# Load order of the first batch, load timing of the later ones, and the last stores of a fused attention and expert kernel

## The chip, the cores and the metric

The kernel runs on one core of a Trainium2 chip. The metric is the time of one execution in device microseconds (us); lower is better. Two kinds of number appear: the **time** of plain executions (a median of several), and the **span** of one profiled execution, from its first instruction to its last, about 2 us shorter. The sets of rounds ran on different chips, so a kernel is compared with the kernel before of its own set where that is possible.

PE is the matmul engine and PEld its weight loads, DVE the vector engine, ACT the scalar engine, POOL the general engine whose queue issues the loads, SP the engine whose queue issues DMA transposes and stores.

## The reference

Four batches of cross-covariance attention (queries and keys are normalised along the sequence, so the attention matrix is 256 x 256), followed by a feed-forward network without activation functions:

```python
B, N, C = (4, 5824, 256)
qn = q / (np.linalg.norm(q, axis=1, keepdims=True) + 1e-06)
kn = k / (np.linalg.norm(k, axis=1, keepdims=True) + 1e-06)
s = kn.transpose(0, 2, 1) @ qn / tau
a = softmax(s)                      # over the last axis
x = (v @ a).reshape(B * N, C)
h = ((x @ w1) * (x @ w2)) @ w3      # d_ff = 1024
out = h @ w_out
```

(The softmax is shortened here.) The kernel folds `a` into w1 and w2 once for each batch (the "folds", giving `Wf`), and w3 into w_out once (`W_sb`), so that the long part is two products `a` and `b` of v with `Wf`, their elementwise product, and one output product `o`.

## The kernel before

The engines' programs are laid out by hand: Python code puts steps on an agenda by a model clock (`at(t, cost, fn)`), and each engine executes its own list in order. A wait on one engine holds back everything behind it on that engine.

The first batch has nothing to overlap with. Its loads all go through POOL's queue, and PE does squares (for the norms) and products (for G) as pieces land:

```python
for pi in range(1, 4):
    load_piece("k", 0, pi)
    load_piece("q", 0, pi)
load_piece("k", 0, 4)
load_piece("k", 0, 5)
# ... PE: squares and products of pieces 0 to 3
load_piece("q", 0, 4, (half,))
load_piece("q", 0, 5, (2, 4))
for h in range(2):                  # expert weights, by halves of their columns
    nc.gpsimd.dma_start(out=w12[:, :, 0, hs], in_=w1r[:, :, hs])
    nc.gpsimd.dma_start(out=w12[:, :, 1, hs], in_=w2r[:, :, hs])
    # ... half h of v piece 0
squares("k", 4, whole)
squares("k", 5, range(LAST + 1), end=True)
soft0[0]()                          # DVE: diagonal of k's squares
busy(2)
soft0[1]()                          # the k row: PE, then four ACT steps
# ... PE: squares and products of q pieces 4 and 5, softmax up to e
soft0[3]()
busy(4)                             # warm-up matmuls, into the wait for e
transpose_half_on_pe(0, 0, 0, False)
soft0[4]()                          # row sums of e, folds 0 to 5
```

In the later batches loads and transposes lie on the agenda. `gate` makes POOL wait for current work of PE, ACT and DVE, and `hold` makes it wait for a DMA transpose of v; `hold` is used only in batch 0:

```python
moves = [("v", b, 3, 1.0), ("qk", n, 0, 4.0), ("qk", n, 1, 12.0), ...]
if before is not None and b == 0:
    at(t, 0.0, lambda w=before: hold(...))
at(t, 0.0, gate)
```

The last, small chunk of a batch has one tile of 128 rows and, in every second batch, a second one with the 64 left-over rows of two batches. Both go into one PSUM tile:

```python
nc.scalar.copy(o[:, 0, :], tl[0][:, 0, :])
(nc.scalar if b == B - 1 else nc.sync).dma_start(out=rows[:, NT - 1, :], in_=o[:, 0, :])
if b % 2 == 1:
    nc.vector.tensor_copy(o[:, 1, :], tl[0][:, 1, :])
    for k in range(2):
        nc.sync.dma_start(out=..., in_=o[k * LEFT : (k + 1) * LEFT, 1, :])
```

Of the kernel before, what the change touches and what calls it, by code (L numbers as in the profile page):

```python
# [12 lines left out]
F32 = DT.float32  # L13
BF16 = DT.bfloat16

P = 128
# [8 lines left out]
def kernel(  # L25
# [12 lines left out]
    nc = tc.nc  # L38

    B, N, C = q.shape  # L40
    T, D = out.shape
# [8 lines left out]
    FT = F // P  # L50
    NT = N // P
    LEFT = N - NT * P
    assert LEFT == 64 and NT % 4 == 1
    NP_ = (NT + PIECE - 1) // PIECE
    LAST = NT - (NP_ - 1) * PIECE
# [57 lines left out]
    def load_piece(nm, n, pi, cuts=()):  # L113

        new_piece(nm, n, pi)
        ends = [0, *cuts, LAST if pi == NP_ - 1 else PIECE]
        for lo, hi in zip(ends, ends[1:]):
            load_part(nm, n, pi, lo, hi)
# [86 lines left out]
    def busy(k):  # L205

        m = psum.tile([P, 512], F32, tag="ab", name=f"warm_{nc.get_next_instruction_name()}", bufs=4)
        for _ in range(k):
            nc.tensor.matmul(m, lhsT=warm[:, :P], rhs=warm, start=True, stop=True, skip_group_check=True)
# [29 lines left out]
    def soft_units(n):  # L239
# [94 lines left out]
            sum_mm(0)  # L334
            sum_mm(1)

        def fold_mm(i, c2, tag="ab"):
            h, rest = divmod(i, 4)
            w, c1 = divmod(rest, 2)
            if c2 == 0:  # L340
                st["fold", i] = psum.tile(
                    [P, 512], F32, tag=tag, name=f"fold_{n}_{i}", bufs={"ab": 4, "out": 3}[tag]
                )
            nc.tensor.matmul(  # L344
                st["fold", i], lhsT=st["e"][:, c2, c1 * P : (c1 + 1) * P], rhs=w12[:, c2, w, h * 512 : (h + 1) * 512],
                start=(c2 == 0), stop=(c2 == CT - 1),
            )
            if c2 == CT - 1:
                dst = Wf[n][:, c1, w, h * 512 : (h + 1) * 512]
                if i % 2 == 0:  # L350
                    nc.scalar.activation(out=dst, in_=st["fold", i], func=AF.Copy, scale=st["rs"][:, c1 : c1 + 1])  # L351
                else:
                    nc.vector.tensor_scalar_mul(dst, st["fold", i], st["rs"][:, c1 : c1 + 1])

        def fold(i, tag="ab"):
            fold_mm(i, 0, tag)
            fold_mm(i, 1, tag)

        def first_folds():
            sum_mm(0)  # L360
            fold_mm(0, 0)
            fold_mm(1, 0)
            sum_mm(1)
            fold_mm(0, 1)
            fold_mm(1, 1)
            fold(2)
            fold(3)
            fold(4, "out")
            fold(5, "out")

        if n == 0:
# [17 lines left out]
    def at(t, cost, fn):  # L389
        seq[0] += 1  # L390
        agenda.append((t, seq[0], cost, fn))
# [57 lines left out]
    def emit_out(b, c, j, ab):  # L449
        small = c == NCH - 1  # L450
        if small:
            lhs = [ab[:, :P]]
            if b % 2 == 1:
                lhs.append(lefts[b // 2][:, j, :, :].rearrange("p b t -> p (b t)"))
        else:
            lhs = [ab[:, i * P : (i + 1) * P] for i in range(4)]
        if j == 0:
            out_tiles[b, c] = [
                psum.tile([P, 2, D], F32, tag="out", name=f"o_{b}_{c}_{h}", bufs=3) for h in range((len(lhs) + 1) // 2)
            ]  # L460
        tl = out_tiles[b, c]
        for s, lhsT in enumerate(lhs):
            nc.tensor.matmul(  # L463
                tl[s // 2][:, s % 2, :], lhsT=lhsT, rhs=W_sb[:, j, :],
                start=(j == 0 and s % 2 == 0), stop=(j == FT - 1 and (s % 2 == 1 or s == len(lhs) - 1)),
                skip_group_check=True,
            )
        clock[0] += len(lhs) * (D * MM_COL + MM_FIX)
        if j == FT - 1:
            o = work.tile([P, 4, D], F32, tag="o_sb", name=f"osb_{b}_{c}", bufs=3)  # L470
            rows = out[b * N : b * N + NT * P, :].rearrange("(p i) c -> p i c", i=NT)
            if small:
                nc.scalar.copy(o[:, 0, :], tl[0][:, 0, :])
                (nc.scalar if b == B - 1 else nc.sync).dma_start(out=rows[:, NT - 1, :], in_=o[:, 0, :])
                if b % 2 == 1:
                    nc.vector.tensor_copy(o[:, 1, :], tl[0][:, 1, :])
                    for k in range(2):
                        m = b - 1 + k
                        nc.sync.dma_start(
                            out=out[m * N + NT * P : (m + 1) * N, :], in_=o[k * LEFT : (k + 1) * LEFT, 1, :]  # L480
                        )
            else:
                nc.scalar.copy(o[:, 0:2, :], tl[0])  # L483
                nc.vector.tensor_copy(o[:, 2:4, :], tl[1])  # L484
                nc.sync.dma_start(out=rows[:, 4 * c : 4 * c + 4, :], in_=o)
            del out_tiles[b, c]
# [8 lines left out]
    half = PIECE // 2  # L495
# [20 lines left out]
    for pi in range(1, 4):  # L516
        load_piece("k", 0, pi)
        load_piece("q", 0, pi)
    load_piece("k", 0, 4)
    load_piece("k", 0, 5)  # L520
    soft0 = soft_units(0)
    whole = range(PIECE)
# [6 lines left out]
        products(0, sl)  # L529
    for pi in range(1, 4):  # L530
        squares("k", pi, whole)
        busy(2)
        squares("q", pi, whole)
        products(pi, whole)
    load_piece("q", 0, 4, (half,))
    load_piece("q", 0, 5, (2, 4))
    for h in range(2):
        hs = slice(h * F // 2, (h + 1) * F // 2)
        nc.gpsimd.dma_start(out=w12[:, :, 0, hs], in_=w1r[:, :, hs])
# [6 lines left out]
    nc.gpsimd.dma_start(out=wout_sb, in_=moe_w_out.rearrange("(lh ll) c -> ll lh c", ll=P))  # L546
    nc.gpsimd.dma_start(out=w3_bf, in_=w3r)
    squares("k", 4, whole)
    squares("k", 5, range(LAST + 1), end=True)
    soft0[0]()  # L550
    busy(2)
    soft0[1]()
    for sl in (lo, hi):
        squares("q", 4, sl)
        products(4, sl)
    parts = [[LAST, 0, 1], [2, 3], [4]]
    for sl in parts:
        squares("q", 5, sl, end=sl is parts[-1])
        if sl is parts[-1]:
            soft0[2]()  # L560
        products(5, sl, end=sl is parts[-1])
    soft0[3]()
    busy(4)
    transpose_half_on_pe(0, 0, 0, False)
    soft0[4]()
    w_ready = [False]

# [15 lines left out]
    def make_agenda(b):  # L583
        agenda.clear()
        clock[0] = 0.0
        n = b + 1
        if b == 0:
            for i in range(2):
                at(1.5 + 0.6 * i, 0.43, soft0[5 + i])
            at(4.0, 0.5, lambda: transpose_half_on_pe(0, 0, 1, False))  # L590
            at(7.0, 0.5, lambda: transpose_half_on_pe(0, 1, 0, True))
            at(8.0, 0.5, lambda: transpose_half_on_pe(0, 1, 1, False))
            at(15.0, 0.0, transpose_w3)
            at(15.0, 0.0, lambda: transpose_piece(0, 2))
            for jt in range(FT):
                at(26.0 + 1.2 * jt, 0.87, lambda jt=jt: w_unit(jt))
            moves = [("v", 0, 3, 29.0), ("qk", 1, 0, 38.0), ("qk", 1, 1, 43.0), ("v", 0, 4, 50.0), ("qk", 1, 2, 58.0)]
            moves += [("qk", 1, 3, 63.0), ("v", 0, 5, 70.0), ("qk", 1, 4, 81.0), ("qk", 1, 5, 87.0)]
            moves += [("v", 1, 0, 96.0), ("v", 1, 1, 106.0), ("v", 1, 2, 116.0)]
            t0, t1 = 58.0, 120.0  # L600
        else:
            moves = [("v", b, 3, 1.0), ("qk", n, 0, 4.0), ("qk", n, 1, 12.0), ("v", b, 4, 20.0), ("qk", n, 2, 27.0)]
            moves += [("v", b, 5, 34.0), ("qk", n, 3, 44.0), ("qk", n, 4, 58.0), ("qk", n, 5, 72.0)]
            moves += [("v", n, 0, 84.0), ("v", n, 1, 96.0), ("v", n, 2, 108.0)]
            moves = [m for m in moves if m[1] < B]
            t0, t1 = 16.0, 104.0


        before = (0, 2) if b == 0 else None
        for nm, m, pi, t in moves:  # L610
            if before is not None and b == 0:
                at(t, 0.0, lambda w=before: hold(vTs[w[0]][1][:1, 0, :1] if w[1] == NP_ - 1 else vTs[w[0]][0][:1, w[1] * PIECE, 0, :1]))
            at(t, 0.0, gate)
            if nm == "qk":
                at(t, 0.0, lambda m=m, pi=pi: load_qk(m, pi))
                before = None
            else:
                at(t, 0.0, lambda m=m, pi=pi: load_piece("v", m, pi))
                at(t + (4.0 if b == 0 else 8.0), 0.0, lambda m=m, pi=pi: transpose_piece(m, pi))
                before = (m, pi)  # L620
        if n == B:
            agenda.sort()
            return
        units = score_units(n)
        for i, (cst, fn) in enumerate(units):
            at(t0 + (t1 - t0) * i / len(units), cst, fn)
        soft = soft_units(n)
        ts = [t1 + 1.0, t1 + 3.5, t1 + 4.0, t1 + 8.0, t1 + 12.0] + [t1 + 13.0 + 0.9 * i for i in range(8)]
        for t, (cst, fn) in zip(ts, soft):
            at(t, cst, fn)  # L630
        agenda.sort()
# [50 lines left out]
```

## Time and profile before

| quantity | value |
|---|---|
| time, median of 3 | 576.39 us (576.14 to 577.7) |
| span of the profile | 574.4 us |
| PE busy | 561.9 us, 98% |
| PE idle between 40 and 569 us | 0.86 us |
| first `a` matmul on the chain of waits | 40.66 us |
| last matmul begins / span ends | 569.59 / 574.4 us |

Most of a profile like this one, here 529 of 574 us, can be put aside at once: where the engine that sets the pace (PE) is busy without a gap, only taking work from it helps. What is left lies at the two ends. The prediction below shows the lines.

### The profile page before, as it was taken

How to read it: one execution, taken by the hardware profiler on the slowest of the kernel's cores; microseconds unless marked ns; L12 is line 12 of the kernel's file. 1: busy time of each engine (PE TensorE's matmuls, PEld its weight loads, DVE VectorE, ACT ScalarE, POOL GpSimd, SP SyncE). 2: the span in 40 equal slices, each digit the busy share in tenths (PEclk: the TensorE clock that was granted, in tenths of full speed). 3: DMA queues.
4: the chain of work that ended last, by engine and by line, in shares of the span. 5: the costliest groups of instructions: out<-in, count | busy, mean ns of one | idle time of the engine just before them, and what ended most of it. 6: DMA issues, size and time to landing. Idle time of an engine off the chain costs nothing.

```text
span 574.4 us, 10119 instructions
## 1 busy us (share of the span) xinstructions
PE 561.9 (98%) x3770; PEld 356.8 (62%) x3770; DVE 374.7 (65%) x597; ACT 338.6 (59%) x624; POOL 65.9 (11%) x147
## 2 busy tenths in 40 slices
PE   7899999999999999999999999999999999999996
PEld 4665576776666666666666666666665656666665
DVE  0047744687967567887776567778876655565564
ACT  0046534777766567776765567767765554454453
POOL 5240020302100212010000112001100000000000
PEclk9999999999999999999999999999999999999999
DMA  8999959879570997564643798654562335311011
GB/s 163 211 208 201 186 101 229 178 167 218 129 182 38 174 210 154 111 149 90 143 111 88 142 226 173 139 111 100 136 143 78 84 80 145 83 45 67 38 74 55
DMA packets 74416, 76.93 MB, mean 134 GB/s; under 512 B 54144, under 2 KB 58112, under 8 KB 74368
## 3 DMA queue, kind: packets, MB, share of 16 engines
q0 software_dynamic: 15360, 39.46, 39.5%
q1 hardware_dynamic: 58864, 36.71, 21.8%
q8 instruction: 29, 0.48, 0.3%
q14 instruction: 19, 0.16, 0.1%
q10 hardware_dynamic: 144, 0.13, 0.1%
HBM read 78.91 MB, written 23.86 MB: 179 GB/s over the span
## 4 chain that ended last, share of the span: by engine, by line
PE 90%; DMA 6%; ACT 1%; issue 1%; DVE 1%; POOL 1%; ACTq 0%; POOLq 0%
PE o L463 27%; PE a L424 27%; PE b L424 27%; PE G L188 5%; DMA q<-in_q_dram 4%; PE fold L344 2%; PE w L571 1%; DMA v<-in_v_dram 1%; ACT as L430 1%; POOL k L109 0%; DVE abs L439 0%; DVE osb L484 0%; PE row L272 0%; POOL q L109 0%; PE ss L283 0%
## 5 line engine op out<-in xcount | busy, mean ns | idle before, releaser
L439 DVE TENSOR_TENSOR abs<-as,b 128x512 bf16<-128x512 bf16 x336 | 229.9, 687 | 140.1 <-ACT as L430 128.6
L430 ACT CAST as<-a 128x512 bf16<-128x512 f32 (+1 forms) x384 | 215.8, 563 | 176.4 <-PE a L424 86.1
L424 PEld LDWEIGHTS <-Wf 128*128 128x128 bf16 x1536 | 149.1, 98 | 102.1 <-issue 2.3
L463 PE MATMUL o<-W_sb,abs 128*128 128x256 bf16 x1376 | 209.7, 273 | 0.5 <-ACT osb L483 0.4
L424 PE MATMUL a<-vT,Wf 128*128 128x512 bf16 x704 | 209.3, 379 | 0.3
L424 PE MATMUL b<-vT,Wf 128*128 128x512 bf16 x704 | 209.4, 379 | 0.0
L463 PEld LDWEIGHTS <-abs 128*128 128x128 bf16 x1376 | 134.5, 98 | 82.0 <-issue 0.6
L197 DVE TENSOR_TENSOR acc<-acc,sq 128x1024 f32<-128x1024 f32 x66 | 80.5, 1219 | 0.8 <-ACT sq L185 0.8
L188 PE MATMUL G<-k,q 128*128 128x256 bf16 x276 | 49.6, 273 | 0.0
L412 POOL COPY gate_t<-abs 1x1 bf16<-1x1 bf16 x39 | 9.7, 249 | 299.0 <-DVE abs L439 290.5
L185 ACT ACTIVATE sq<-q 128x512 f32<-128x512 bf16 x66 | 41.8, 633 | 0.0
L185 ACT ACTIVATE sq<-k 128x512 f32<-128x512 bf16 x66 | 41.6, 631 | 0.0
L484 DVE COPY osb<-o 128x512 f32<-128x512 f32 x44 | 30.1, 685 | 0.0
L188 PEld LDWEIGHTS <-q 128*128 128x128 bf16 x276 | 27.0, 98 | 3.1
L483 ACT COPY osb<-o 128x512 f32<-128x512 f32 x44 | 25.8, 586 | 4.5 <-PE o L463 2.6
L274 ACT ACTIVATE kr<-row 128x256 f32<-128x256 f32 x4 | 1.5, 384 | 31.2 <-PE row L272 31.2
L344 PE MATMUL fold<-w,e 128*128 128x512 bf16 x64 | 16.8, 378 | 0.0
L109 POOL DMA_DIRECT2D q<-in_q_dram x28 | 15.1, 539 | 14.2 <-DMA k<-in_k_dram 5.4
L351 ACT ACTIVATE Wf<-fold,rs 128x512 bf16<-128x512 f32 x16 | 10.9, 687 | 7.2 <-PE fold L344 4.9
L109 POOL DMA_DIRECT2D k<-in_k_dram x25 | 13.7, 549 | 3.4 <-DMA k<-in_k_dram 1.9
L109 POOL DMA_DIRECT2D v<-in_v_dram x25 | 13.5, 540 | 5.7 <-issue 3.9
L439 DVE TENSOR_TENSOR abq<-as,b 128x512 bf16<-128x512 bf16 x16 | 10.9, 686 | 3.9 <-ACT as L430 3.4
(89 smaller groups left out, 209.7 us busy)
## 6 DMA issues: line engine op xcount, KB each, us to landing
out_dram<-osb SPq DMA_DIRECT2D x44, 512.0 KB, 3.1
k<-in_k_dram POOLq DMA_DIRECT2D x19, 512.0 KB, 8.8
v<-in_v_dram POOLq DMA_DIRECT2D x19, 512.0 KB, 5.2
q<-in_q_dram POOLq DMA_DIRECT2D x18, 512.0 KB, 6.3
w_wout<-in_moe_w_dram POOLq DMA_DIRECT2D x1, 2048.0 KB, 22.2
k<-in_k_dram POOLq DMA_DIRECT2D x4, 320.0 KB, 8.9
v<-in_v_dram POOLq DMA_DIRECT2D x4, 320.0 KB, 5.2
q<-in_q_dram POOLq DMA_DIRECT2D x4, 256.0 KB, 10.5
```

Of the source, the lines that this page charges most:

```text
L109: nc.gpsimd.dma_start(out=pieces[nm, n, pi][:, lo:hi, :], in_=qk_main[nm, n][0][:, pi * PIECE + lo : pi * PIECE + hi, :])
L185: nc.scalar.activation(out=dst[:, :, part, :], in_=src[:, o : o + 2, :], func=AF.Square)
L188: nc.tensor.matmul(G[:, ct, :], lhsT=qt[:, i, ct * P : (ct + 1) * P], rhs=kt[:, i, :], start=(pr == 0 and part == 0 and ct == 0), stop=(pr ...
L197: nc.vector.tensor_add(accs[n], accs[n], sqs[0])
L344: nc.tensor.matmul(st["fold", i], lhsT=st["e"][:, c2, c1 * P : (c1 + 1) * P], rhs=w12[:, c2, w, h * 512 : (h + 1) * 512], start=(c2 == 0), ...
L351: nc.scalar.activation(out=dst, in_=st["fold", i], func=AF.Copy, scale=st["rs"][:, c1 : c1 + 1])
L424: nc.tensor.matmul(t[:, :n], lhsT=Wf[b][:, ct, w, j * P : (j + 1) * P], rhs=rhs_of(b, c, ct), start=(ct == 0), stop=(ct == CT - 1),)
L430: nc.scalar.copy(a_sb[:, :n], tiles[0][:, :n])
L439: nc.vector.tensor_mul(ab, a_sb, tiles[1])
L463: nc.tensor.matmul(tl[s // 2][:, s % 2, :], lhsT=lhsT, rhs=W_sb[:, j, :], start=(j == 0 and s % 2 == 0), stop=(j == FT - 1 and (s % 2 == 1 ...
L483: nc.scalar.copy(o[:, 0:2, :], tl[0])
L484: nc.vector.tensor_copy(o[:, 2:4, :], tl[1])
```

## The change

The intent: get through the first batch's data sooner by taking q and k in turn to the end; keep loads and DMA transposes of the later batches apart; and shorten the way from the last matmul to the last store. The diff, cut (marked with `...`) to its core:

```diff
         def first_folds():
...
             fold(2)
-            fold(3)
-            fold(4, "out")
+            transpose_half_on_pe(0, 0, 0, False)
+            fold(3, on_act=True)
+            fold(4, "out", on_act=False)
             fold(5, "out")
...
-                psum.tile([P, 2, D], F32, tag="out", name=f"o_{b}_{c}_{h}", bufs=3) for h in range((len(lhs) + 1) // 2)
+                psum.tile([P, 2, D], F32, tag="out", name=f"o_{b}_{c}_{h}", bufs=3)
+                for h in range(len(lhs) if small else 2)
...
-                    nc.vector.tensor_copy(o[:, 1, :], tl[0][:, 1, :])
-                    for k in range(2):
+                    o2 = work.tile([P, D], F32, tag="kr", name=f"oleft_{b}", bufs=1)
+                    nc.vector.tensor_copy(o2, tl[1][:, 0, :])
+                    for k, eng in enumerate((nc.sync, other)):
...
     load_piece("k", 0, 4)
+    load_piece("q", 0, 4, (half,))
     load_piece("k", 0, 5)
...
-    load_piece("q", 0, 4, (half,))
-    load_piece("q", 0, 5, (2, 4))
+    load_piece("q", 0, 5, (1, 3, 4))
...
     squares("k", 4, whole)
-    squares("k", 5, range(LAST + 1), end=True)
-    soft0[0]()
-    busy(2)
-    soft0[1]()
     for sl in (lo, hi):
         squares("q", 4, sl)
         products(4, sl)
-    parts = [[LAST, 0, 1], [2, 3], [4]]
+    squares("k", 5, range(LAST + 1), end=True)
+    soft0[0]()
+    parts = [[LAST, 0], [1, 2], [3], [4]]
...
+        if i == 0:
+            soft0[1]()
     soft0[3]()
     busy(4)
-    transpose_half_on_pe(0, 0, 0, False)
     soft0[4]()
...
-            if before is not None and b == 0:
+            if before is not None:
                 at(t, 0.0, lambda w=before: hold(...))
...
-                at(t + (4.0 if b == 0 else 8.0), 0.0, lambda m=m, pi=pi: transpose_piece(m, pi))
+                at(t + 4.0, 0.0, lambda m=m, pi=pi: transpose_piece(m, pi))
```

In the lists of moves for the later batches, `("qk", n + 1, 0, 108.0)` is added at the end of batch b, and the other loads move by up to 12 us.

More of the change, by code (lines that the diff above doesn't have):

```diff
@@ L335, in sums, with fold_mm @@
             sum_mm(1)
-        def fold_mm(i, c2, tag="ab"):
+        def fold_mm(i, c2, tag="ab", on_act=None):
             h, rest = divmod(i, 4)
@@ L349, in fold_mm @@
                 dst = Wf[n][:, c1, w, h * 512 : (h + 1) * 512]
-                if i % 2 == 0:
+                if on_act if on_act is not None else i % 2 == 0:
                     nc.scalar.activation(out=dst, in_=st["fold", i], func=AF.Copy, scale=st["rs"][:, c1 : c1 + 1])
@@ L353, in fold_mm, with fold @@
                     nc.vector.tensor_scalar_mul(dst, st["fold", i], st["rs"][:, c1 : c1 + 1])
-        def fold(i, tag="ab"):
+        def fold(i, tag="ab", on_act=None):
             fold_mm(i, 0, tag)
-            fold_mm(i, 1, tag)
+            fold_mm(i, 1, tag, i % 2 == 0 if on_act is None else on_act)
         def first_folds():
@@ L462, in emit_out @@
         for s, lhsT in enumerate(lhs):
+            h, o = (s, 0) if small else divmod(s, 2)
             nc.tensor.matmul(
-                tl[s // 2][:, s % 2, :], lhsT=lhsT, rhs=W_sb[:, j, :],
-                start=(j == 0 and s % 2 == 0), stop=(j == FT - 1 and (s % 2 == 1 or s == len(lhs) - 1)),
+                tl[h][:, o, :], lhsT=lhsT, rhs=W_sb[:, j, :],
+                start=(j == 0 and o == 0), stop=(j == FT - 1 and (small or o == 1)),
                 skip_group_check=True,
@@ L473, in emit_out @@
                 nc.scalar.copy(o[:, 0, :], tl[0][:, 0, :])
-                (nc.scalar if b == B - 1 else nc.sync).dma_start(out=rows[:, NT - 1, :], in_=o[:, 0, :])
+                other = nc.scalar if b == B - 1 else nc.sync
+                other.dma_start(out=rows[:, NT - 1, :], in_=o[:, 0, :])
                 if b % 2 == 1:
-                    nc.vector.tensor_copy(o[:, 1, :], tl[0][:, 1, :])
-                    for k in range(2):
+                    o2 = work.tile([P, D], F32, tag="kr", name=f"oleft_{b}", bufs=1)
+                    nc.vector.tensor_copy(o2, tl[1][:, 0, :])
+                    for k, eng in enumerate((nc.sync, other)):
                         m = b - 1 + k
-                        nc.sync.dma_start(
-                            out=out[m * N + NT * P : (m + 1) * N, :], in_=o[k * LEFT : (k + 1) * LEFT, 1, :]
-                        )
+                        eng.dma_start(out=out[m * N + NT * P : (m + 1) * N, :], in_=o2[k * LEFT : (k + 1) * LEFT, :])
             else:
@@ L531 @@
         squares("k", pi, whole)
-        busy(2)
+        if pi < 3:
+            busy(2)
         squares("q", pi, whole)
         products(pi, whole)
-    load_piece("q", 0, 4, (half,))
-    load_piece("q", 0, 5, (2, 4))
+    load_piece("q", 0, 5, (1, 3, 4))
     for h in range(2):
@@ L548 @@
     squares("k", 4, whole)
-    squares("k", 5, range(LAST + 1), end=True)
-    soft0[0]()
-    busy(2)
-    soft0[1]()
     for sl in (lo, hi):
@@ L555 @@
         products(4, sl)
-    parts = [[LAST, 0, 1], [2, 3], [4]]
-    for sl in parts:
-        squares("q", 5, sl, end=sl is parts[-1])
-        if sl is parts[-1]:
+    squares("k", 5, range(LAST + 1), end=True)
+    soft0[0]()
+    parts = [[LAST, 0], [1, 2], [3], [4]]
+    for i, sl in enumerate(parts):
+        end = i == len(parts) - 1
+        squares("q", 5, sl, end=end)
+        if end:
             soft0[2]()
-        products(5, sl, end=sl is parts[-1])
+        products(5, sl, end=end)
+        if i == 0:
+            soft0[1]()
     soft0[3]()
     busy(4)
-    transpose_half_on_pe(0, 0, 0, False)
     soft0[4]()
@@ L598, in make_agenda @@
             moves += [("qk", 1, 3, 63.0), ("v", 0, 5, 70.0), ("qk", 1, 4, 81.0), ("qk", 1, 5, 87.0)]
-            moves += [("v", 1, 0, 96.0), ("v", 1, 1, 106.0), ("v", 1, 2, 116.0)]
+            moves += [("v", 1, 0, 96.0), ("v", 1, 1, 106.0), ("v", 1, 2, 116.0), ("qk", 2, 0, 126.0)]
             t0, t1 = 58.0, 120.0
         else:
-            moves = [("v", b, 3, 1.0), ("qk", n, 0, 4.0), ("qk", n, 1, 12.0), ("v", b, 4, 20.0), ("qk", n, 2, 27.0)]
-            moves += [("v", b, 5, 34.0), ("qk", n, 3, 44.0), ("qk", n, 4, 58.0), ("qk", n, 5, 72.0)]
-            moves += [("v", n, 0, 84.0), ("v", n, 1, 96.0), ("v", n, 2, 108.0)]
+            moves = [("v", b, 3, 1.0), ("qk", n, 1, 10.0), ("qk", n, 2, 17.0), ("v", b, 4, 26.0), ("qk", n, 3, 38.0)]
+            moves += [("v", b, 5, 46.0), ("qk", n, 4, 58.0), ("qk", n, 5, 66.0)]
+            moves += [("v", n, 0, 76.0), ("v", n, 1, 86.0), ("v", n, 2, 96.0), ("qk", n + 1, 0, 108.0)]
             moves = [m for m in moves if m[1] < B]
```

## The prediction

> **What bounds the kernel now.** I read the busy table first, then busy time by stretch, the waits of the tensor engine, the chain of waits through the first 40 us and the timeline of both ends.
>
> The page's busy table and its slices:
>
> ```profile
> span 574.4 us, 10119 instructions
> PE 561.9 (98%) x3770; PEld 356.8 (62%) x3770; DVE 374.7 (65%) x597; ACT 338.6 (59%) x624; POOL 65.9 (11%) x147
> ...
> PE   7899999999999999999999999999999999999996
> ```
>
> PE is busy in 98% of the span, and only the first and last slices (14.4 us each) fall clearly short. Asking for the busy time of stretches (columns: PE, PEld, DVE, ACT, POOL, granted clock, DMA share, GB/s) puts a number on the middle:
>
> ```profile
> 10.00:20.00 10.00, 6.29 (x75) 4.81 (x72) 0.17 (x1) 0.00 (x0) 1.62 (x3) 1.00 1.06 213
> 40.00:569.00 529.00, 528.14 (x3439) 332.78 (x3436) 368.57 (x573) 332.78 (x613) 48.16 (x112) 1.00 0.59 130
> ```
>
> From 40 to 569 us PE lacks 529.00 - 528.14 = 0.86 us, at clock 1.00. A busy PE need not run at its peak, so I checked the spacing too: in the chain of waits a pair of 128x512 matmuls takes 0.43 us and four 128x256 take 0.44, and summing such spacings for the kinds of this stretch (704 pairs for a and b, 64 pairs with 192 columns at 0.17, 1456 output matmuls at 0.109, 276 for G at 0.109, folds, W products, transposes) gives about 527 us by hand: the stretch is full. So 12.5 us of idle PE in all, of which 1.25 is the start, about 4.5 the end (the last matmul ends near 569.9), and most of the rest waits for loads:
>
> ```profile
> PE sqq L221 <- DMA q<-in_q_dram: 3.6, 4, 1.9
> PE sqk L221 <- DMA k<-in_k_dram: 1.4, 2, 0.9
> ...
> PE tr_I-494_495 L132 <- DMA v<-in_v_dram: 0.6, 1, 0.6
> PE o L463 <- ACT osb L483: 0.4, 1, 0.4
> ```
>
> (Columns: total us, times, longest.) No wait for q, k, v or vT comes from batches 1 to 3. The first 35 us run at the pace of the loads, about 210 GB/s written at a DMA share above 1. Their ends can be dated, because the POOL queue issues each load when the load eight places ahead has landed, and the timeline shows these waits: the main part of k piece 5 lands at 28.95, the halves of q piece 4 at 30.2 and 31.5. The last 64 KB of q piece 5, issued at 27.52 with 5.8 us to landing, land at 33.3. PE's last product is later:
>
> ```profile
> 35.30 0.38 PE L233 MATMUL G<-k,q 128*128 128x256 bf16 x2
> ...
> 37.16 0.62 PE L132 MATMUL tr_I-494_495<-ident_b,v 128*128 128x128 bf16 x8 [0.62 <-DMA v<-in_v_dram]
> 37.23 0.91 ACT L307 ACTIVATE e<-s,r 128x256 bf16<-128x256 f32 x2 [0.74 <-DVE r L294]
> 37.79 0.20 PE L323 MATMUL sum<-ones_b,e 128*128 128x1 bf16 x2
> ```
>
> PE was 2 us behind the data, because q4 and q5 arrived after k5 and all their squares and products piled up. Then a softmax tail of about 1.8 us leads to e at 37.23, sums at 37.79, and from 38.3 PE never stops. The end:
>
> ```profile
> 569.46 0.28 PE L463 MATMUL o<-W_sb,abs 128*128 128x256 bf16 x1
> 569.91 0.37 ACT L473 COPY osb<-o 128x256 f32<-128x256 f32 x1 [0.83 <-PE o L463]
> 570.32 0.42 DVE L476 COPY osb<-o 128x256 f32<-128x256 f32 x1 [0.78 <-ACT osb L473]
> 570.77 1.12 SPq L479 DMA_DIRECT2D out_dram<-osb  x2
> ```
>
> DVE's copy waits for ACT's, then SP issues two stores one behind the other, and the span ends at 574.4.
>
> **What the Trainium skill says.** "TensorE: Matmul & The Clock Gate", section "Back-to-back issue gap", gives N/2.4 + 2.5 ns when warm, 216 ns for 512 columns; the chain's 0.43 us a pair agrees (the 131 ns it also names for sustained streams does not appear). "PSUM — Partial Sum Buffer", section "PSUM bank collisions raise a hardware error", says that software must keep two engines off one bank, two readers included; that fits the 0.78 us in which DVE waits for an ACT copy of other columns of the same tile. "DMA: Bandwidth & Descriptors", section "Issuing engines are not separate DMA queues", says that issuing from several engines saves only sequencer time: here that is the second half of the 1.12 us above. The same page, "Rules for kernel authors", says a DMA transpose beside ordinary DMAs needs nothing; batches 1 to 3 already run so without a PE wait.
>
> **The change, part by part.**
>
> 1. *Load order of the first batch.* k4, q4, k5, q5 in place of k4, k5, q4, q5; bytes are equal, so the last still lands near 33.2. At 2.45 us a piece from k4's landing at 27.2: q4's halves at 28.4 and 29.7, k5 at 31.4, then q5's slots, now cut 1/2/1/1, to 33.2. PE does q4's work (8 slots of 0.11 + 0.22 us = 2.6 us) while k5 loads, is done by about 31.1, squares k5 from 31.4 to 32.2, takes q5's first part to 32.8, and the k row follows to 33.4. The rest ends near 34.6, in place of 35.6. But the k row moves back: it ran at 30.36 and its four ACT steps ended at 32.93 (1.83 us, hidden); now they run from about 33.5 to 35.4, and q's Ln and Exp queue behind them. Then 0.4 (scale) + 0.7 (r) + 0.4 (second scale) leads to e near 36.6. **Estimate: e 0.6 us earlier**, not 1.
>
> 2. *v transpose behind fold 2.* It filled a wait for e (ended 37.78, sums at 37.79), so it cost almost nothing. Between folds it costs its 0.45 us of PE (chain of waits). It no longer blocks the folds if v is late, but v lands at 37.1 in both orders, since no bytes move across it. Fold copies change engine so that DVE is free for the vT copy: at 0.7 us each they end about when a and b need them. **+0.45. The head nets about -0.2 us.** The warm-up matmuls taken out lay in waits: 0.
>
> 3. *Last chunk's outputs in a PSUM tile each.* ACT's copy waits for one matmul less (0.1 us), DVE's starts near 569.9, not 570.32 (0.4), and the second small store goes out on the ACT queue, not behind the first (0.56). The last issue would end near 571.0 in place of 571.9. **-0.8 us**, with the landing time unchanged. The added tile takes a buffer that ACT's copy of chunk 10 frees: in batch 1 that copy ends at 314.13 and the matmul is due near 314.16, so a wait of 0 to 0.1 us.
>
> 4. *Batches 1 to 3: loads held for transposes, transposes 4 us sooner, piece 0 of the next q and k a batch early.* These move transfers in a stretch where PE waits for none. q and k of each piece keep at least 14 us between due load and use (due 17, used about 47 for piece 2), and every issue lands in 3 to 11 us by the DMA table. **0.** It removes a risk, and no time.
>
> Sum: -0.2 - 0.8 + 0.1 = about -1 us, or **575.4** from 576.39.
>
> **The rivals.**
> - *PE catches up wholly in the head.* Had k's row stayed off the path, e could start at 33.2 + 0.5 + 1.8 = 35.5 and the head would win 1.3 us net: about 574.3 in all. For it: 2 us of PE backlog. Against: k5 is now nearly last and its row takes 1.8 us of ACT.
> - *The hold becomes the wait.* POOL stands still on a transpose, SP on a load, and SP also issues the output stores, with three osb buffers. A wait of more than some 20 us there would stop ACT and then PE, for 577 or more. In batch 0, where holds are already there, the longest takes 35.1 us on POOL and PE still does not stop, so this is unlikely.
> - *The head loses.* If the k chain slips by another 0.5 us, or folds 4 and 5 wait for w's second half (due near 38.3, used near 39.5), the moved transpose makes the head a loss of up to 0.5 us: 576.
>
> **Range and chances.** The three runs of before spread from 576.14 to 577.7, as large as the effect. Rivals give 574.3 to 577; I take 574.1 to 576.6. Everything outside the 40-to-569 stretch's work is 12.5 us of idle PE, 2.2% of the span, so faster by over 2% needs nearly all of it gone: 0.01. Slower by over 2% needs 11.5 us of new waits: 0.01.
>
> **What would show it.** Step 1: last product near 34.6, e near 36.6, the row's ACT work ending just before. Step 2: first a matmul near 40.3 (now 40.49). Step 3: DVE's last copy beginning with ACT's, and at most 3.5 us from the last matmul to the end (now 4.5). Step 4: PE lacking under 1.5 us between 40 and 569, with POOL's waits on vT grown. A new PE wait on vT or osb, or on q in a later batch, would make it wrong.

## The result, and the profile after

The changed kernel took 575.43 us (median of 4, 575.43 to 575.97); the kernel before, with one more run beside it, 576.72 us (median of 4, 576.14 to 577.7). The ratio is 0.9978, with a 95% interval of 0.9961 to 0.9996. Ratios here are the mean time of one kernel's fast runs over that of the other's fast runs of the same rounds, so they are not quite the ratio of the medians. In a later set of five rounds the changed kernel, as a control, took 575.50 against 576.24, ratio 0.9988 (0.9974 to 1.0001). By the medians the gain is therefore 0.7 to 1.3 us, or 0.1 to 0.2%; the second interval just includes no gain.

The page of the changed kernel: busy time and the slices of PE.

```profile
span 573.6 us, 10125 instructions
PE 561.9 (98%) x3760; PEld 357.0 (62%) x3766; DVE 374.1 (65%) x597; ACT 337.9 (59%) x624; POOL 71.0 (12%) x162
```

PE does the same 561.9 us of work; the span is 0.8 shorter. Busy time between 40 and 569 us (columns: length, PE, PEld, DVE, ACT, POOL, clock, DMA share, GB/s):

```profile
40.00:569.00 529.00, 527.95 (x3434) 332.59 (x3435) 368.43 (x573) 331.45 (x612) 52.83 (x126) 1.00 0.58 131
```

There PE now lacks 1.05 us, not 0.86: the middle did not get better. The timeline of the head:

```profile
34.76 0.38 PE L233 MATMUL G<-k,q 128*128 128x256 bf16 x2
...
36.44 0.91 ACT L307 ACTIVATE e<-s,r 128x256 bf16<-128x256 f32 x2 [0.44 <-DVE r L294]
...
37.00 0.20 PE L323 MATMUL sum<-ones_b,e 128*128 128x1 bf16 x2 [1.00 <-ACT e L307]
...
38.41 0.61 PE L132 MATMUL tr_I-508_509<-ident_b,v 128*128 128x128 bf16 x8
...
40.15 0.59 PE L425 MATMUL a<-vT,Wf 128*128 128x512 bf16 x2
```

G is done 0.54 us sooner and e begins 0.79 us sooner, but the first `a` only 0.34 us sooner (40.15, before 40.49). PE now stands still for 1.00 us before the sums, and the transpose that used to lie in this wait comes later, between the folds. And the timeline of the end:

```profile
569.59 0.28 PE L466 MATMUL o<-W_sb,left 128*128 128x256 bf16 x1
569.78 0.37 ACT L476 COPY osb<-o 128x256 f32<-128x256 f32 x1 [0.70 <-PE o L466]
569.91 0.42 DVE L481 COPY oleft<-o 128x256 f32<-128x256 f32 x1 [0.38 <-PE o L466]
570.18 0.38 ACTq L478 DMA_DIRECT2D out_dram<-osb  x1
570.37 0.49 SPq L484 DMA_DIRECT2D out_dram<-oleft  x1
570.60 0.53 ACTq L484 DMA_DIRECT2D out_dram<-oleft  x1
```

The last matmul begins at 569.59, as in the kernel before. The lead of 0.34 us with which `a` began is gone by then. The span is shorter only because everything behind that matmul is. Walking along the chain shows where the lead went: it is 0.35 us up to 313 us, in the small chunk of batch 1 it falls to 0.17, and in the small chunk of batch 3 to zero. The timeline there, first the kernel before, then the changed one:

```profile
565.53 0.59 ACT L483 COPY osb<-o 128x512 f32<-128x512 f32 x1
...
565.88 0.27 PE L463 MATMUL o<-W_sb,abs 128*128 128x256 bf16 x1
...
565.99 0.27 PE L463 MATMUL o<-W_sb,left 128*128 128x256 bf16 x1
```

```profile
565.36 0.58 ACT L486 COPY osb<-o 128x512 f32<-128x512 f32 x1
...
565.70 0.27 PE L466 MATMUL o<-W_sb,abs 128*128 128x256 bf16 x1
...
565.99 0.27 PE L466 MATMUL o<-W_sb,left 128*128 128x256 bf16 x1
```

Before, the matmul on the left-over rows follows its neighbour by 0.11 us. Now it follows by 0.29: it begins 0.05 after ACT's copy ends (565.36 + 0.58 = 565.94). My reading at this point: the added PSUM tile takes a buffer that this copy has to empty, and costs 0.18 us each time.

### The profile page after: what moved, and what is told of

The parts are those of the page before. It is cut to its first block, busy times and chain, and to the rows that moved or that the text cites. A ratio compares the mean times of both kernels' runs of the same rounds, so it can differ in the third digit from the quotient of the medians.

```text
span 573.6 us, 10125 instructions
## 1 busy us (share of the span) xinstructions
PE 561.9 (98%) x3760; PEld 357.0 (62%) x3766; DVE 374.1 (65%) x597; ACT 337.9 (59%) x624; POOL 71.0 (12%) x162
## 4 chain that ended last, share of the span: by engine, by line
PE 91%; DMA 5%; ACT 1%; issue 1%; DVE 1%; POOL 1%; ACTq 0%; POOLq 0%
PE o L466 27%; PE a L425 27%; PE b L425 27%; PE G L188 5%; DMA k<-in_k_dram 3%; PE fold L344 2%; DMA q<-in_q_dram 2%; PE w L575 1%; ACT as L431 1%; POOL k L109 0%; PE row L272 0%; POOL q L109 0%; DVE abs L440 0%; DVE osb L487 0%; ACT kr L276 0%
## 5 line engine op out<-in xcount | busy, mean ns | idle before, releaser
L413 POOL COPY gate_t<-abs 1x1 bf16<-1x1 bf16 x39 | 12.1, 310 | 183.7 <-DVE abs L440 183.1
L417 POOL COPY gate_t<-vT 1x1 bf16<-1x1 bf16 x17 | 4.0, 234 | 180.5 <-DMA vT<-v 145.1
```

The costliest lines, as they stand in the source:

```text
L413: nc.gpsimd.tensor_copy(gate_t, last_ab[0][:1, :1])
```

## The experiments

My theory, A: head, middle and end add up. The span is (start of `a`) + (PE's work up to the last matmul: 529.2 us, plus 0.35 for two waits at the added PSUM tile) + (end behind it: 4.5 us before, 3.7 after). The rivals: the moved loads carry part of the gain; the waits come from something else; the end is set by landing times that no queue changes. Twelve runs tell these apart.

This table holds the three terms for each run, from one profile each: the start of `a` on the chain of waits (about 0.17 us later than in the timeline), the time from there to the end of the last matmul (its start in the timeline plus 0.28), and from there to the end of the span; then medians of time, and the ratio to the kernel before in the same set.

| run | `a` starts | to last matmul's end | to the end | span | time | before | ratio |
|---|---|---|---|---|---|---|---|
| kernel before | 40.66 | 529.21 | 4.5 | 574.4 | | | |
| changed kernel | 40.32 | 529.55 | 3.7 | 573.6 | 575.43 | 576.72 | 0.9978 |
| e_head | 40.69 | 529.32 | 4.5 | 574.5 | 576.60 | 576.28 | 1.0005 |
| e_out | 40.43 | 529.61 | 3.8 | 573.8 | 575.66 | 576.28 | 0.9987 |
| e_moves | 40.83 | 529.17 | 4.5 | 574.5 | 576.01 | 576.28 | 0.9993 |
| e_tr_early | 40.98 | 529.52 | 3.8 | 574.3 | 575.60 | 576.28 | 0.9987 |
| e_bank | 40.88 | 529.18 | 3.7 | 573.8 | 575.41 | 576.02 | 0.9987 |
| e_onebank | 40.68 | 529.17 | 4.15 | 574.0 | 575.48 | 576.02 | 0.9990 |
| e_oneq | 40.41 | 529.54 | 4.15 | 574.1 | 575.79 | 576.02 | 0.9991 |
| e_late | 39.96 | 529.53 | 3.7 | 573.2 | 575.63 | 576.02 | 0.9987 |
| e_again (changed kernel) | 40.73 | 529.55 | 3.8 | 574.1 | 575.50 | 576.24 | 0.9988 |
| e_v_first | 39.95 | 529.54 | 3.8 | 573.3 | 575.53 | 576.24 | 0.9988 |
| e_best | 39.31 | 530.09 | 3.8 | 573.2 | 574.88 | 576.24 | 0.9977 |
| e_best2 | 39.11 | 530.09 | 3.8 | 573.0 | 574.74 | 576.40 | 0.9965 |

(In e_best and e_best2 two folds, 0.87 us, lie behind the first `a` matmuls, so their second term is 529.22 without them.) The second and third columns fall into two groups each, to within 0.1 us. The first column does not: the same head gives 39.96 to 40.88, because the first loads do not land at the same time in each execution. A timed difference below about 0.5 us is not resolved by five rounds here.

### One part of the change at a time

**e_head**: only the changed head in the kernel before (this edit and the next two are given in words; their lines are those of the diff above).

```diff
 kernel before
+ load order k4 q4 k5 q5, k row behind q5's first part, v transpose behind fold 2, fold copies on other engines
```

> The kernel before with the changed head alone (load order, cuts of q piece 5, place of the k row, v transpose behind fold 2, fold copies on other engines). Theory A (head and tail are separate, nothing in between matters): first a matmul at 40.15 us as in the changed kernel (40.49 before), this lead of 0.34 kept to the last matmul, which ends near 569.53, and a span of 574.4 - 0.34 = 574.1. Rival B (the lead is swallowed in later batches by waits for loads or by softmax stretches): the last matmul ends at 569.87 as before, span 574.4.

Measured: `a` at 40.69, span 574.5, ratio 1.0005 (0.9993 to 1.0018): no gain. Not for rival B's reason, since the second term is 529.32, about that of the kernel before: nothing swallowed the lead later. There was no lead. e began at 36.20, even sooner than in the changed kernel, and then PE waited in front of fold 4:

```profile
PE sum L323 <- ACT e L307: 1.0, 1, 1.0
PE fold L344 <- DMA w<-in_moe_w_dram: 0.4, 1, 0.4
```

So the head has a further limit that the first profile of the changed kernel hardly shows: the second half of the expert weights. The control shows it as well (PE weight loads in the timeline; in brackets the idle time ahead and what ended it):

```profile
38.71 0.15 PEld L344 LDWEIGHTS <-e 128*128 128x128 bf16 x2
39.69 0.33 PEld L344 LDWEIGHTS <-e 128*128 128x128 bf16 x3 [0.83 <-DMA w<-in_moe_w_dram]
```

(PE's own wait at this place, 0.34 us, the profile puts down to DVE's vT copy, which ended at 39.66, as w landed. It was w: in e_bank fold 4 began at 39.84, while that copy ran on to 40.04.)

In the seven profiles with the changed head as it stands, the time from e to `a` is 3.88 us in three (the changed kernel, e_oneq, e_late) and 4.14 to 4.49 in four. In the three, that weight load waits some 0.3 us for w, beside the fold ahead of it; in the four it waits 0.58 to 0.93 us, and PE stands still. With the old head it is 3.43 in all three.

This limit comes with the changed head. With the old load order the part of w that fold 4 needs (the second half of w1's columns) is issued at 31.77 and lands 6.6 us later, at 38.40 (38.22 to 38.64 in three profiles). With the new order it lands at 39.18 in the changed kernel, and at 38.87 to 39.79 in the eight profiles whose v and w are queued in the same order; the means are 38.42 and 39.38, about 1.0 us apart, although the same bytes lie ahead of it and the last of q lands at the same time (means 33.32 and 33.38). Between 34.6 and 38.4 us the DMA engines move less (kernel before, then changed kernel; the last column is GB/s):

```profile
34.60:38.40 3.80, 3.17 (x32) 1.97 (x31) 2.38 (x9) 1.32 (x4) 1.97 (x3) 1.00 1.20 204
```

```profile
34.60:38.40 3.80, 2.75 (x19) 1.34 (x19) 2.03 (x11) 2.43 (x8) 2.40 (x4) 1.00 1.08 168
```

It is 203 to 206 GB/s in all three profiles with the old order and 160 to 182 in all eleven with the new one. Which part of the changed head does this (the order, the one issue more for q piece 5, or what runs beside the loads) no run separates; it stays open.

**e_out**: only the output of the small chunk.

```diff
 kernel before
+ own PSUM tile and own SBUF tile for the left-over rows, second small store on ACT's queue
```

> The kernel before with the changed output of the small last chunk alone (own PSUM tile for the left-over rows, second small store on the ACT queue). Theory A: the added tile costs two waits of 0.17 us (batches 1 and 3), so the last matmul ends 0.34 later, near 570.2; DVE's copy then starts 0.04 after it (0.45 before), the end follows the last matmul by 3.7 us in place of 4.5: span 574.4 + 0.34 - 0.8 = 573.95. Rival B (the waits are an artefact of the new head's timing): no PE wait, span 573.6.

Measured: second term 529.61 (0.40 longer), third 3.8, span 573.8, ratio 0.9987 (0.9974 to 0.9999). The waits come with this part, with the old head too: rival B falls. The net gain of this part in the profile is 0.7 - 0.4 = 0.3 us, and the rest of this run's shorter span is an early head (40.43).

**e_moves**: only the moved loads.

```diff
 kernel before
+ hold in all batches, transposes 4 us sooner, piece 0 of the next q and k a batch early
```

> The kernel before with the moved loads alone (holds for transposes in all batches, transposes 4 us sooner, piece 0 of the next q and k a batch early). Theory A (PE waits for no load after 40 us, so where loads lie is worth nothing): span 574.4 within 0.1, no new PE wait, POOL's waits for vT up from about 90 to about 180 us. Rival B (the moves carry part of the gain): 574.0 or less, or if the hold delays stores or loads: over 574.8.

Measured: second term 529.17, against 529.21 before; no PE wait that was not there before; span 574.5; ratio 0.9993 (0.9979 to 1.0006). POOL's waits, of the kernel before and then of this run (columns: total us, times, longest):

```profile
POOL gate_t L416 <- DMA vT<-v: 75.6, 5, 35.1
...
POOL gate_t L416 <- DMA vTt<-v: 16.0, 1, 16.0
```

```profile
POOL gate_t L416 <- DMA vT<-v: 178.7, 17, 35.1
POOL gate_t L416 <- DMA vTt<-v: 33.9, 3, 15.9
```

POOL waits 121 us more for transposes (and 106 us less at `gate`: 184.2 in place of 290.5), and PE does not notice. The part does what it says and is worth nothing in time, as theory A has it.

**e_late**: the changed kernel, with every load and transpose of batches 1 to 3 begun 8 us later.

```diff
-            moves = [m for m in moves if m[1] < B]
+            moves = [(nm, m, pi, t + 8.0) for nm, m, pi, t in moves if m < B]
```

> The changed kernel with every load and transpose of batches 1 to 3 begun 8 us later in the schedule. Theory A (these transfers have slack and are off the path): no new PE wait, span 573.6 within 0.1. Rival B (the earlier start and the holds are what keeps PE fed): PE waits for q, k or vT appear, span over 574.5.

Measured: second term 529.53, as in the changed kernel; no new PE wait. The span of 573.2 is outside my 0.1, and shorter; the whole difference is the first column (39.96), which lies ahead of the first load that was moved. The edit stands in the list for the agendas of batches 1 to 3, so the first loads of batch 1, which lie on batch 0's agenda, did not move; in the trace the transfers from 187 us on are issued 6 to 9 us later. They have at least some 6 us of slack: rival B falls for them.

### The end

**e_bank**: the changed kernel, with the left-over rows' PSUM tile in G's buffer.

```diff
                 psum.tile([P, 2, D], F32, tag="out", name=f"o_{b}_{c}_{h}", bufs=3)
+                if not (small and h == 1) else psum.tile([P, CT, C], F32, tag="G", name=f"o_{b}_{c}_{h}", bufs=1)
                 for h in range(len(lhs) if small else 2)
```

> The changed kernel, with the left-over rows' PSUM tile taken not from the three output buffers but from the buffer of G, which is free by then. Theory A (the two waits of 0.17 us in batches 1 and 3 are waits for ACT's copy out of the buffer that the added tile takes): both waits vanish, the head's lead of 0.34 reaches the end, last matmul near 569.53, span 573.6 - 0.34 = 573.25. Rival B (the waits come from something else in that chunk, such as ACT's or DVE's own load): the waits stay, span 573.6.

Measured: the second term is back at 529.18, so both waits are gone, and the matmul on the left-over rows follows its neighbour by 0.11 us again (batch 1, timeline):

```profile
314.07 0.27 PE L467 MATMUL o<-W_sb,abs 128*128 128x256 bf16 x1
314.18 0.27 PE L467 MATMUL o<-W_sb,left 128*128 128x256 bf16 x1
```

That settles the waits: it was the buffer. The span of 573.8 missed my 573.25 because the loads landed late in this execution (`a` at 40.88, waiting for w).

**e_onebank**: the changed kernel, both small outputs in one PSUM tile again, but with separate SBUF tiles and two queues.

```diff
-                    nc.vector.tensor_copy(o2, tl[1][:, 0, :])
+                    nc.vector.tensor_copy(o2, tl[0][:, 1, :])
```

(with the tile's allocation and matmul indices as in the kernel before)

> The changed kernel with both small outputs in one PSUM tile again, as before, but with the two queues and the separate SBUF tile of the left-over rows. Theory A (DVE waited for ACT because both read one tile): no added buffer, so last matmul near 569.53 (0.34 earlier than changed), but ACT's copy starts after both matmuls and DVE's copy starts when ACT's ends, 0.41 later after the last matmul: span about 573.6 - 0.34 + 0.41 = 573.7. Rival B (DVE waited because both copies wrote one SBUF tile, which is separate here): DVE starts with ACT, span about 573.25.

Measured: second term 529.17, third 4.15. DVE waits for ACT again, although the two write different SBUF tiles:

```profile
569.89 0.37 ACT L476 COPY osb<-o 128x256 f32<-128x256 f32 x1 [0.83 <-PE o L466]
...
570.29 0.42 DVE L481 COPY oleft<-o 128x256 f32<-128x256 f32 x1 [0.78 <-ACT osb L476]
```

So it is the shared PSUM tile (theory A), and it costs 4.15 - 3.73 = 0.42 us (the spans are read to 0.1 us; DVE's start alone moves by 0.40, from 0.04 to 0.44 us after the last matmul's end).

**e_oneq**: the changed kernel, both left-over stores on SP's queue.

```diff
-                    for k, eng in enumerate((nc.sync, other)):
+                    for k, eng in enumerate((nc.sync, nc.sync)):
```

> The changed kernel with both left-over stores on the SP queue, one behind the other, as before. Theory A (the last issue sets the end; two queues save one issue of about 0.55 us, less the 0.2 that ACT's own first issue costs): the last issue ends at about 571.45 in place of 571.13, span 573.6 + 0.3 = 573.9. Rival B (the end is set by landing of the large store or by something after the queues): span 573.6.

Measured: third term 4.15 in place of 3.73; span 574.1 (expected 573.9). The second queue is worth about 0.4 us: the timeline has the two issues on SP as one group of 1.12 us from 570.44, to 571.56, which is 1.6 us after the last matmul's end, against 1.26 with two queues (571.13 - 569.87).

### The head

**e_tr_early**: the changed kernel, with the v transpose back in front of the sums.

```diff
             fold(2)
-            transpose_half_on_pe(0, 0, 0, False)
             fold(3, on_act=True)
...
     busy(4)
+    transpose_half_on_pe(0, 0, 0, False)
     soft0[4]()
```

> The changed kernel with the v transpose put back ahead of the sums and folds; fold copies stay as changed. In the changed kernel PE waits 1.0 us for e before the sums (from 36.0 to 37.0), so the place of the transpose could be free if v had landed. Theory A (v's first half lands near 37.1 as before, since no byte ahead of it changed): the transpose waits for v until about 37.1, the sums start near 37.6 and a near 40.3 to 40.4, so 0.0 to 0.2 us slower than the changed kernel: the move behind fold 2 was worth at most that. Rival B (v lands earlier in the new order): the transpose hides in the wait, a at 39.7, 0.45 us faster.

Measured: the transpose waited for v:

```profile
PE tr_I-487_488 L132 <- DMA v<-in_v_dram: 1.8, 1, 1.8
```

It ran at 37.66, and e to `a` took 4.41 us. Theory A's mechanism holds, its size does not: v landed at 37.62, not 37.1, and `a` came 0.66 us later than in the changed kernel's first profile (40.98 against 40.32). But 4.41 lies within the 3.88 to 4.49 of the changed head, so it is not shown that moving the transpose behind fold 2 gained anything. What kept it out of the wait for e is v's place in the queue.

**e_v_first**: as e_tr_early, and v's first half loaded ahead of the expert weights.

```diff
+    new_piece("v", 0, 0)
+    load_part("v", 0, 0, 0, half)
     for h in range(2):
         hs = slice(h * F // 2, (h + 1) * F // 2)
...
-        if h == 0:
-            new_piece("v", 0, 0)
-        load_part("v", 0, 0, h * half, (h + 1) * half)
+        if h == 1:
+            load_part("v", 0, 0, h * half, (h + 1) * half)
```

> The changed kernel with v's first half loaded ahead of the expert weights and its transpose put back ahead of the sums, into PE's wait for e. Theory A (in the head PE has 1.0 us of idle time before the sums, and only v's landing kept the transpose out of it): the transpose runs near 35.9 without a wait, 0.45 us of PE leave the path, but folds 4 and 5 then come up near 38.6 to 38.9, and the weights' second half lands only near 39.2, so a PE wait of 0.3 to 0.6 us for w appears and a starts near 40.2: gain 0 to 0.3 us. Rival B (w lands in time): a at 39.9 and no wait for w. Rival C (w's first half is now late for folds 0 to 3): slower than the changed kernel.

Measured: the transpose ran in the wait for e, without a wait of its own, and e to `a` is 3.42 us: 0.46 less than the best of the changed head.

```profile
35.50 0.61 PE L132 MATMUL tr_I-487_488<-ident_b,v 128*128 128x128 bf16 x8
...
37.09 0.20 PE L323 MATMUL sum<-ones_b,e 128*128 128x1 bf16 x2 [0.98 <-ACT e L307]
```

The wait for w that I expected did not come in this profile (rival B); w landed at 38.49. In four others with the same bytes ahead of it, it landed only at 39.6 to 39.8. Why it varies so is open. The time, 575.53 against 575.50 for the control, shows no gain; the five runs spread from 575.01 to 576.32.

**e_best**: v first, the k row ahead of q5's first part, folds 4 and 5 behind the first `a` and `b` matmuls (so that they come after w has landed), and G's buffer for the left-over rows.

```diff
+            mid = [lambda: fold(4, "out", on_act=False), lambda: fold(5, "out")]
...
             tiles.append(t)
+            if (b, c, j) == (0, 0, 0):
+                soft0[7 + w]()
...
     soft0[0]()
+    soft0[1]()
     parts = [[LAST, 0], [1, 2], [3], [4]]
```

(with the edits of e_bank and e_v_first; the copy of fold 3 goes back to DVE)

> All mends together: v's first half ahead of the weights and transposed in PE's wait, the k row's matmuls ahead of q5's first part, folds 4 and 5 behind the first a and b group so that they need not wait for the second half of w, and the left-over rows' PSUM tile in G's buffer. Theory A: the first a on PE near 39.0 (40.15 to 40.7 now; 0.87 of this is only the two folds moved behind it), PE without a gap from 39 on except 0.3 at the first b, the two waits of 0.17 gone; last matmul near 569.0, span 572.7, against 573.6 for the changed kernel. Rival B (the head is bound by the landing of the last q and the softmax behind it, so the reordering of PE's work gains nothing): only the 0.35 of the PSUM tile, span 573.25.

Measured: 574.88 us (574.81 to 575.05), ratio 0.9977 (0.9965 to 0.9990), in the same set in which the changed kernel took 575.50 (575.35 to 575.82): it beats both, and none of its five runs is as slow as the fastest of the control. Span 573.2 (expected 572.7). One mend did harm: PE waited 0.5 us for DVE's diagonal of k in front of the row, and e came at 36.74.

**e_best2**: e_best with the k row back behind q5's first part.

> The version with all mends, but with the k row's matmuls back behind the first part of q piece 5, as in the changed kernel. In the version with the row first PE waited 0.52 us for DVE's diagonal of k before the row, and q's last squares and products ended 0.5 us later (35.12 against 34.15 to 34.81), so e came at 36.74 against 36.08 to 36.74 elsewhere. Theory A (the row first only shifts the wait; q's end and the row's ACT chain are now about equally late): e near 36.4, first a near 38.95, span 572.9, time 0.2 to 0.4 us under the version with the row first. Rival B (the landing of the loads differs by more from run to run than this is worth): no difference beyond 0.2 us in the median.

Measured: 574.74 us (574.60 to 574.92) against 576.40 for the kernel before in its set, ratio 0.9965 (0.9951 to 0.9979); span 573.0.

```profile
39.11 0.52 PE a L422 x2
39.63 0.43 PE fold L344 x2
40.07 0.43 PE b L422 x2
40.50 0.43 PE fold L344 x2
```

These pieces of its chain show the first `a`, fold 4, `b` and fold 5 without a gap. The difference to e_best, 0.14 us in the medians, is within rival B's 0.2; the place of the k row is not settled by time. This is the best version I have: 0.76 us under the changed kernel's control by the medians, though from another set of rounds, on another chip.

## Why the prediction was right

**The total.** Predicted 575.4 in 574.1 to 576.6; measured 575.43, with a gain of about 1 us. The reasoning that only the ends could pay was right; the terms did not each come out as said: in the head e came earlier than I said and the weights later, which cancelled, and the added buffer cost more. By the profiles the sum is 0.5 us, not 1, so that the time agrees to 0.03 us is in part luck.

**Step 3, the stores: -0.8 predicted, -0.77 measured** (third term 4.5 against 3.73), and by the parts named: about 0.4 each for the separate PSUM tile (e_onebank) and the second queue (e_oneq). Each was undone by itself, so the two overlap a little. The 0.78 us that the prediction gives as DVE's wait for ACT's copy is all of DVE's idle time before its own; only the last 0.4 us of it is that copy, which is what step 3 reckoned with. The sign named beforehand, at most 3.5 us from the last matmul to the end, was stricter than the sum itself (4.5 - 0.8 = 3.7) and was missed.

**Step 3, the added buffer: mis-sized.** I put it at "a wait of 0 to 0.1 us" in batch 1. It is 0.18 us, and twice: 0.35 in all (e_bank). The error is one of reading. I compared the end of ACT's copy, 314.13, from the timeline, with the matmul's due time of 314.16 from the chain of waits, which counts 0.17 us later. In one view, the timeline, the matmul was due at 313.99, and 314.13 + 0.05 - 313.99 = 0.19 would have stood there to be read. I also left out that batch 3 has the same chunk.

**Steps 1 and 2, the head: right in sum, not in its terms.** I predicted e 0.6 us earlier and `a` 0.2. Over the profiles, e begins at 37.00 to 37.40 with the old head (three, mean 37.21) and at 36.08 to 36.74 with the changed one (eight, with e_tr_early; mean 36.39): 0.8 earlier. `a` starts at 40.64 on average (three) and 40.52 (seven): 0.1 earlier. The price of the transpose behind fold 2 was 0.45, as said (3.88 against 3.43 from e to `a`). What I had only as a possibility, folds 4 and 5 waiting for w's second half, happens in four of seven profiles and takes another 0.26 to 0.61 us. This is where the head's working was wrong: "v lands at 37.1 in both orders, since no bytes move across it" held for the order of the bytes and not for their time. v landed at 37.10 on average with the old order and at 37.48 with the new one, and w, which the prediction had due near 38.3, at 39.38. The rival in which PE catches up wholly and wins 1.3 us did not come true: the k row's ACT steps end only 0.76 us before e begins (35.26 + 0.42 = 35.68, and 36.44).

**Step 4, the loads: 0 predicted, 0 measured** (e_moves, 0.04 us in the second term; e_late, at least some 6 us of slack for the transfers that it moved).

By the profiles the changed kernel's gain is then 0.1 (head, on average) + 0.77 (stores) - 0.35 (added buffer) = about 0.5 us. The timed gain, 0.7 in the larger set, agrees within the scatter of the runs. The first set's 1.3 us owes something to two long runs of the kernel before (577.7 and 577.05); the set of e_best2 has three such (577.35 to 577.95), so its ratio rests partly on them.

## What to carry to other kernels

Split a span into the part where the bound engine has no gap and the parts before and after it, and price a change in each part by itself. If the ends are all there is, one more buffer taken from a rotating set can give back as much as the head gained: ask what empties that buffer, and when, and read both times in the same view. Where an engine waits for a result, look for work that could lie in the wait, and then for the load that keeps it out; here one load's place in the queue was worth 0.45 us on the path, and the reordering of the first batch 0.1. A new order of loads can also change when later loads land, though none of their bytes moved: read the landing again after the change.

## What the Trainium skill lacked or had wrong

- "PSUM — Partial Sum Buffer", section "PSUM bank collisions raise a hardware error": it says that engines must be kept apart on one bank, but gives no cost for doing so. Here two copies of different columns of one tile cost 0.42 us more than copies from two tiles (4.15 against 3.73 us to the end), and the second tile, taken from the rotating buffers, cost 0.18 us each time it had to be emptied first.
- "TensorE: Matmul & The Clock Gate", section "Back-to-back issue gap": the sustained 131 ns for a matmul of 512 columns does not appear; all profiles here show 0.43 us for a pair, about 215 ns each, close to the 216 ns that the page gives for a matmul by itself.
- No page that I read says how far the landing of the same loads varies between executions: with the same head code, the first `a` began between 39.96 and 40.88 us, and the part of the expert weights that fold 4 needs landed up to 0.9 us apart (38.87 to 39.79).
